# One-hots made one step ahead, checks spread anew, and rows of y written by ScalarE and completed by accumulating transfers

## The chip, the cores and the metric

One core of one Trainium2 chip runs the kernel. The metric is the device time of one execution in microseconds (us). Five engines work side by side, each through its own queue in order: TensorE (PE; its weight loads are PEld), VectorE (DVE), ScalarE (ACT), GpSimd (POOL) and SyncE (SP). SP here only issues transfers (DMAs), also in order: a transfer that waits holds up every later one of SP.

## The reference

```python
xn = _layernorm(x)                       # x: 2048 x 512
out = x + A(xn) + B(xn)

# A: Fourier mixing, y = Cr @ (xn @ Wr^T) - Ci @ (xn @ Wi^T)

# B: product-key experts, 32 heads, 64 x 64 = 4096 experts, 2 of them per head
q = einsum("nd,dhc->nhc", xn, w_q);  s1 = q1 @ k1^T;  s2 = q2 @ k2^T
# top 2 of s1 and of s2, top 2 of their 4 sums; g = softmax over the 2
act = gelu(einsum("nd,nhkd->nhk", xn, u[top_e]))
out_B = einsum("nhk,nhk,nhkd->nd", g, act, v[top_e])
```

## The kernel before

The 2048 rows are 16 blocks of 128. Up to about 455 us of the span the kernel computes part A (its rows go to a buffer y_d in HBM), the scores and the routing. The change lies in what follows: the experts, computed densely. For every block b there are three kinds of work on TensorE:

- **z** (phases ("z", ...), lines 1108 and 1186): xn times all of u, transposed, 128 experts at a time. From block 2 on two blocks go together, in 28 slots of 24 short matmuls (`SEQ`, `slot`). A slot's result lies in one of four shared PSUM banks. ScalarE copies it out (lines 1225, 1230, 1232) or VectorE adds it to what lies in `ACT[b]` (lines 1227, 1235, 1238); the bank is free after that. Gelu follows at line 1215. Part of the weights are sums that stream from HBM through a ring of three slots (`ring_load`, line 1169): when a slot has been read for the last time, SP loads the next 512 KB into it.
- **g** (`g_mm`, line 1289): the gates of the chosen experts, spread to a 128 x 4096 array, in four groups of 32 rows per block. A group has two halves of 16 rows. For each half VectorE makes a one-hot L (line 1279, the low 7 bits of the expert's number) and a one-hot R (line 1284, the high bits) and multiplies R by the gate (line 1287); then 16 matmuls L x R write the bank. L and R have three buffers, taken in turn.
- **v** (phases ("v", b), line 1349): the products times v, 96 long matmuls in eight groups (`cg`) of twelve, all into one bank `pv`. Between them `w_part` (lines 1297 to 1305) forms the next block's products of gates, gelu and scale and splits them into two halves of float16. Seven of sixteen pieces of v stream from HBM (`v_load`, line 1325).

At the end of a block `add_x` has SP load the block's row of part A from y_d into the tile y (line 1359), and GpSimd's queue add x to it with an accumulating transfer (line 1360). `finish` has VectorE compute y = pv * scale + y (line 1364) and SP store y to the output (line 1365). y has one buffer. The last block is finished in `v_part` itself (lines 1331 to 1341), in two halves.

Beside that run **checks** that C and the other given matrices have the structure that part A used. `U` is a step of them: such a step runs what earlier steps left (`later`, `loaded`) and issues the next unit's loads. A unit of C loads 512 KB (lines 1377, 1378), one step later VectorE sums the magnitudes of the first 128 columns (line 1385) and forms differences (lines 1391 to 1429), one step later ScalarE sums the magnitudes of the differences (line 1430). `F[0]` and `F[1]` are steps of another check, `fit`. `verdict`, in the last block, reduces it all to a flag.

Where each piece stands is written by hand: `put(phase, group, ...)` puts it behind a group of matmuls of a phase. This source order is not yet the order of the queues: the framework's planner orders each engine's instructions by priority and by when it expects their inputs. An instruction wrapped in `pin` (`keep_in_program_order`) stays behind the instruction that precedes it in the source on its engine. Waits on semaphores are then set by the framework.

Of the kernel before, what the change touches and what calls it, by code (L numbers as in the profile page):

```python
# [7 lines left out]
F32 = mybir.dt.float32  # L8
# [6 lines left out]
AF = mybir.ActivationFunctionType  # L15
ALU = mybir.AluOpType
AX = mybir.AxisListType

P = 128
S = 2048  # L20
D = 512
KD = D // P
NT = S // P
# [13 lines left out]
def tile_fnet_peer(ctx, tc, x, ca, cb, c5, wt, wf, wr, wq, kt, ut, vn, out):  # L37
# [9 lines left out]
    nc = tc.nc  # L47

    dram = ctx.enter_context(tc.tile_pool(name="dram", bufs=1, space=bass.MemoryType.DRAM))
    y_d = dram.tile([NT, P, D], F32, name="y_d")  # L50
# [43 lines left out]
    chk, asum = sums_sb[:, 0:71], sums_sb[:, 71:139]  # L94
# [12 lines left out]
    zsc, fw, osc = scl[:, 0:1], scl[:, 1:2], scl[:, 2:3]  # L107
# [188 lines left out]
    G = (1, 0, 2, 3)  # L296
# [424 lines left out]
    def part_b(safe, stS, stP, stQ, stE, xt, u_sb, cmp_p, w4):  # L721
# [360 lines left out]
        bp = stE.enter_context(tc.tile_pool(name="bp", bufs=2, side="left"))  # L1082
# [175 lines left out]
            return work, middle, behind  # L1258

        GP = {}  # L1260

        def parts(b):

# [1 line left out]
            return act.rearrange("p c n -> p (c n)").bitcast(F16).rearrange(  # L1265
                "p (c n l) -> p c n l", c=NC, l=2)

        def g_mm(b, tg):
            cmp = CMP[b]
            p = pg(f"g{b}_{tg}")  # L1270
            for hf in range(2):
                ts = slice(tg * TG + hf * 16, tg * TG + hf * 16 + 16)

                def bc(w, n):
                    return cmp[:, w, ts, :].unsqueeze(2).to_broadcast([P, 16, n // 2, 2])

                LR.append(LR.pop(0))
                L, R = LR[-1]
                nc.vector.tensor_tensor(  # L1279
                    L.rearrange("p t (l two) -> p t l two", two=2),  # L1280
                    io_lam.rearrange("p (l two) -> p l two", two=2).unsqueeze(1).to_broadcast([P, 16, P // 2, 2]),
                    bc(0, P), op=ALU.is_equal)
                Rv = R.rearrange("p t (c two) -> p t c two", two=2)
                nc.vector.tensor_tensor(  # L1284
                    Rv, io_c.rearrange("p (c two) -> p c two", two=2).unsqueeze(1).to_broadcast([P, 16, NC // 2, 2]),
                    bc(1, NC), op=ALU.is_equal)
                nc.vector.tensor_tensor(Rv, Rv, bc(2, NC), op=ALU.mult)  # L1287
                for t in range(16):
                    nc.tensor.matmul(p[:, hf, t * NC:(t + 1) * NC], L[:, t, :], R[:, t, :], start=True, stop=True)  # L1289
            GP[b, tg] = p  # L1290

# [68 lines left out]
            nc.gpsimd.dma_start(y, x[b % 4, b // 4], accum_op=ALU.add)  # L1360

        def finish(b, pv):
            y = Y[b]
            nc.vector.scalar_tensor_tensor(y, pv, osc, y, op0=ALU.mult, op1=ALU.add)
            nc.sync.dma_start(out[b * P:(b + 1) * P], y)

        later, loaded = [], []
        pin = tc.keep_in_program_order

        def compare(n):  # L1370

# [9 lines left out]
        def compare_in(n, t, tf, tv):  # L1381

            ri, g, kk = n // 32, n // 8 % 4, n % 8
            odd = kk // 4
            pin(nc.vector.tensor_reduce(asum[:, n:n + 1], tf[:, :P], axis=AX.X, op=ALU.add,
                                        apply_absolute_value=True))
            sgn = (((1, 1, 1), (-1, 1, -1)), ((-1, -1, 1), (1, -1, -1)))[ri][odd]
            ops = [ALU.subtract if v > 0 else ALU.add for v in sgn]
            op = ops[1]
            if g == 0:  # L1390
                pin(nc.vector.tensor_tensor(tv[:, 1], tv[:, 1], tv[:, 0], op=ops[0]))
                for i in (2, 3):
                    nc.vector.scalar_tensor_tensor(tv[:, i], tv[:, 0], not0, tv[:, i], op0=ALU.mult, op1=ops[i - 1])  # L1393
                f = (-1 if ri else 1) * sgn[1] * sgn[2]
                nc.vector.tensor_tensor(tv[0:1, 3], tv[0:1, 3], tv[0:1, 2],
                                        op=ALU.subtract if f > 0 else ALU.add)
            else:
                sets = {}
                for i, o in enumerate(ops):
                    sets.setdefault(o, []).append(i + 1)  # L1400
                for o, ix in sets.items():
                    sl = slice(ix[0], ix[-1] + 1, ix[1] - ix[0] if len(ix) > 1 else 1)
                    v = tv[:, sl]
                    pin(nc.vector.tensor_tensor(v, v, tv[:, 0:1].to_broadcast([P, len(ix), 256]), op=o))
            m = ALU.add if ri else ALU.subtract

            def mirror(v):

                c = 0 if kk else 1
                nc.vector.tensor_tensor(v[:, 2:4, c:], v[:, 2:4, c:], v[:, 0:2, c:], op=m)  # L1410
                if c:
                    nc.vector.tensor_tensor(v[:, 3, 0:1], v[:, 3, 0:1], v[:, 2, 0:1], op=m)

            if g == 0:
                mirror(t[0:1, 2])
                if odd and ri:

                    nc.vector.tensor_copy(t[0:1, 2, 0:2], t[0:1, 0, 0:2])
                elif odd == ri:
                    if ri:  # L1420
                        nc.vector.memset(t[0:1, 2, 0:2], 0.0)
                    else:
                        v = t[0:1, 2, 0:2].rearrange("p q (c a) -> p (q c) a", a=2)
                        nc.vector.tensor_tensor(v, v, c52.unsqueeze(1).to_broadcast([1, 64, 2]), op=ALU.add)
                    if kk == 0:
                        nc.vector.memset(t[0:1, 2, 2, 0:1], 0.0)
            mirror(t[:, 0])
            if kk == 0:
                nc.vector.memset(t[:, 0, 2, 0:1], 0.0)
            later.append(lambda: pin(nc.scalar.activation(tf[:, P:], tf[:, P:], AF.Abs, accum_out=chk[:, n:n + 1])))  # L1430

        def compare_w(n):

# [135 lines left out]
        def pg(name):  # L1569
            return psg.tile([P, 2, 512], F32, tag="pg", name=name, bufs=2)  # L1570
# [9 lines left out]
        def put(ph, cg, *fs):  # L1580
            plan.setdefault((ph, cg), []).extend(fs)

        def G(b, k):
            return lambda: g_mm(b, k)

        def W(b, k, here=False):
            return lambda: w_part(b, k, here)

# [3 lines left out]
        F = [U(it=it) for it in fit_units]  # L1592
        U = U()
# [10 lines left out]
        for b in range(NT):  # L1604
            ph = ("v", b)
            if b % 2 == 0 and 0 < b < 13:
                nx = phases[phases.index(ph) + 1]
                st = 1 if len(nx) == 2 else 2
                put(ph, 1, G(b + 1, 0))
                put(ph, 3, G(b + 1, 1))  # L1610
                put(ph, 5, W(b + 1, 0))
                put(ph, 7, W(b + 1, 1), G(b + 1, 2))
                put(nx, st, W(b + 1, 2, True), G(b + 1, 3))
                put(nx, 3 * st, W(b + 1, 3, True))
            elif b + 1 < NT:
                for k in range(4):
                    put(ph, 2 * k or b % 2, W(b + 1, k))
                put(ph, b % 2, G(b + 1, 2))
                put(ph, 3, G(b + 1, 3))
        put(("v", 13), 5, G(15, 0))  # L1620
        put(("v", 13), 7, G(15, 1))
        for ph in phases[2:]:
            if ph[0] == "z":
                put(ph, 9, G(ph[1], 0))
                put(ph, 12, G(ph[1], 1))
        for b in range(13):
            put(("v", b), 3, lambda b=b: compact_d(b + 2))
        put(("z", 14, 15), 8, lambda: compact_d(15))
        if not safe:
            for cg in (1, 3, 5, 7):  # L1630
                put(("v", 0), cg, F[0])
            for ph, cg in ((("v", 12), 0), (("v", 14), 1), (("v", 14), 3), (("v", 14), 7)):
                put(ph, cg, F[0])
            for ph in phases[3:]:
                if ph[0] == "z":
                    put(ph, 8, F[0])
                    for cg in {2: (9, 11, 13, 15), 4: (9, 11, 13, 15), 6: (9, 11, 13, 15), 14: (9, 12)}.get(ph[1], (9, 12, 15)):
                        put(ph, cg, U)
                elif ph[1] < 14:
                    for cg, f in enumerate((None, F[1], F[1], U, U, U, U, F[0]) if ph[1] % 2 == 0 else (  # L1640
                            None, F[1], F[0], None, U, U, U, F[0])):
                        if f and (ph[1] < 13 or f != U):
                            put(ph, cg, f)
            for cg in range(3):
                put(("v", 14), cg, F[1])
                put(("v", 14 + cg // 2), (6, 7, 0)[cg], U)
                put(("v", 15), cg, F[1])
            for f, n in ((U, 68), (F[0], NK + 16 - V2), (F[1], 16 + V2)):
                assert sum(v.count(f) for v in plan.values()) >= n
# [14 lines left out]
        for n, ph in enumerate(phases):  # L1664
            if ph[0] == "z":
                b = ph[1:]
# [14 lines left out]
            b = ph[1]  # L1681
# [8 lines left out]
            for cg in range(8):  # L1690
# [3 lines left out]
                if b + 1 == NT and cg == 3 and not safe:  # L1694
                    step(None)
                    add_x(b)
                    verdict()
            if b + 1 < NT or safe:
                add_x(b)
            else:  # L1700
                ret = nc.values_load(flags, min_val=0, max_val=1)
            if b + 1 < NT or safe:
                finish(b, pv)
# [150 lines left out]
```

## Time and profile before

| | |
|---|---|
| median of 3 runs | 1131.35 us (1128.64 to 1136.68) |
| profiled execution, its own time | 1135.25 us |
| its span, first to last instruction | 1133.4 us |
| granted TensorE clock, mean | 0.995 |
| busy: PE / DVE / ACT / POOL | 98% / 85% / 59% / 29% of the span |
| HBM read / written | 183.06 MB / 29.69 MB |

The profile is of one execution. A group of instructions is given by its line, engine, operation and the tiles that it writes and reads. An engine's idle time stands before the instruction that ended it, with what released that instruction. The stages that matter below are pairs of blocks in the second half of the span.

### The profile page before, as it was taken

The page shows a single profiled execution, that of the slowest core. Times are in us where ns is not written, and L with a number is a line of the kernel's source. Part 1 is how long each engine was busy: PE and PEld are TensorE (multiplying, and loading weights), DVE is VectorE, ACT ScalarE, POOL GpSimd, SP SyncE. Part 2 cuts the span into 40 slices and gives each one's busy share as a digit, 9 for nine tenths or more (in the row PEclk, how much of TensorE's full clock was granted, in tenths as well). Part 3 has the DMA queues.
Part 4 walks back from the last instruction along what each step waited for, and adds up shares of the span by engine and source line. Part 5 has one row for each costly group of instructions (what it writes and reads, how often), then busy time and mean ns, then how long its engine had stood idle before and what let it go on. Part 6 is the DMA issues. An engine that isn't in the chain of part 4 may idle for free.

```text
span 1133.4 us, 29112 instructions
## 1 busy us (share of the span) xinstructions
PE 1107.3 (98%) x11528; PEld 722.5 (64%) x11528; DVE 962.7 (85%) x2904; ACT 663.9 (59%) x1098; POOL 332.7 (29%) x385
## 2 busy tenths in 40 slices
PE   9999999999999999999999999999999999999997
PEld 6455554544545459687488478478569569569643
DVE  7899789999989799948997897898888888888793
ACT  6558598888877584346445545544535545544442
POOL 0429999899888850000000000000000000000000
PEclk9999999999999999999999999999999999999999
DMA  9883546465353335866666777666668668566354
GB/s 291 292 206 148 185 139 223 117 217 170 92 168 96 111 108 191 236 199 205 226 206 226 227 218 241 218 207 232 200 205 263 199 211 269 190 221 206 121 168 134
DMA packets 132273, 220.51 MB, mean 195 GB/s; under 512 B 35092, under 2 KB 71067, under 8 KB 132126
## 3 DMA queue, kind: packets, MB, share of 16 engines
q1 hardware_dynamic: 129520, 214.28, 58.7%
q0 software_dynamic: 2304, 4.20, 2.8%
q8 instruction: 92, 1.51, 0.5%
q14 instruction: 55, 0.45, 0.1%
q10 hardware_dynamic: 302, 0.08, 0.0%
HBM read 183.06 MB, written 29.69 MB: 188 GB/s over the span
## 4 chain that ended last, share of the span: by engine, by line
PE 59%; DVE 15%; DMA 5%; ACT 4%; issue 2%; POOL 1%; SPq 0%; ACTq 0%; DVEq 0%
PE s L252 18%; PE z L1186 17%; PE v L1349 16%; PE z L1108 4%; DMA cx<-in_cb_dram 3%; DVE w L1297 3%; DVE L L1279 3%; PE g L1289 3%; DVE act L1305 2%; PE m L148 1%; DVE R L1287 1%; DVE R L1284 1%; DVE w L1305 1%; DMA s<-s_d 1%; DVE cx L1393 1%
## 5 line engine op out<-in xcount | busy, mean ns | idle before, releaser
L252 PE MATMUL s<-m,xq 128*128 128x512 f16 x1344 | 297.4, 379 | 1.7 <-ACT ss L962 1.4
L1349 PE MATMUL v<-v,act 128*128 128x512 f16 x1044 | 233.3, 379 | 0.0
L252 PEld LDWEIGHTS <-xq 128*128 128x128 f16 x1344 | 129.6, 98 | 153.1 <-issue 3.2
L1360 POOL DMA_DIRECT2D y<-in_x_dram x16 | 14.4, 897 | 658.7 <-DMA v<-v_d 274.7
L1279 DVE TENSOR_TENSOR L<-io_lam,cmp 128x2048 f16<-128x2048 f16 x128 | 156.2, 1221 | 28.1 <-PE g L1289 28.1
L1349 PEld LDWEIGHTS <-act 128*128 128x128 f16 x1044 | 99.2, 98 | 112.4
L1186 PEld LDWEIGHTS <-u 128*128 128x128 f16 x2688 | 156.2, 98 | 14.8 <-issue 8.3
L966 DVE MAX8 vals<-ss 128x8 f32<-128x64 f32 x896 | 133.3, 216 | 5.5 <-ACT ss L962 5.2
L1186 PEld LDWEIGHTS <-s 128*128 128x128 f16 x1944 | 110.6, 98 | 1.2 <-DMA s<-s_d 1.2
L1349 PE MATMUL v<-v,w 128*128 128x512 f16 x480 | 109.0, 384 | 0.0
L1304 ACT ACTIVATE act<-w 128x1024 f16<-128x1024 f32 x36 | 48.9, 1358 | 92.2 <-DVE w L1297 92.2
L970 DVE FIND_INDEX8 idx<-vals,ss 128x8 uint16<-128x256 f32 x224 | 93.7, 418 | 0.0
L962 ACT ACTIVATE ss<-s,wsc 128x512 f32<-128x512 f32 x120 | 80.0, 680 | 22.5 <-PE s L252 12.6
L1186 PE MATMUL z<-xb,u 128*128 128x128 f16 x1344 | 84.9, 220 | 5.3 <-DVE w L1227 4.7
L1186 PE MATMUL z<-x,u 128*128 128x128 f16 x1344 | 84.7, 220 | 1.6 <-DVE act L1238 1.1
L1186 PE MATMUL z<-x,s 128*128 128x128 f16 x1296 | 81.2, 219 | 1.0 <-DMA s<-s_d 1.0
L1215 ACT ACTIVATE act<-act,scl 128x512 f32<-128x512 f32 x56 | 39.6, 720 | 70.9 <-DVE act L1235 40.9
L1349 PEld LDWEIGHTS <-w 128*128 128x128 f16 x480 | 46.1, 99 | 53.1 <-issue 2.3
L1430 ACT ACTIVATE cx<-cx 128x896 f32<-128x896 f32 x64 | 60.0, 938 | 29.6 <-DVE cx L1410 11.7
L1289 PEld LDWEIGHTS <-L 128*128 128x128 f16 x2048 | 60.7, 96 | 17.3 <-issue 7.2
L1289 PE MATMUL g<-R,L 128*128 128x32 f16 x2048 | 63.5, 177 | 6.6 <-DVE R L1287 6.2
L1305 DVE TENSOR_TENSOR act<-w,act 128x1024 f16<-128x1024 f32 x44 | 58.6, 1332 | 6.1 <-ACT act L1304 6.1
(363 smaller groups left out, 1878.9 us busy)
## 6 DMA issues: line engine op xcount, KB each, us to landing
v<-v_d SPq DMA_DIRECT2D x67, 512.0 KB, 4.6
s<-s_d SPq DMA_DIRECT2D x63, 512.0 KB, 4.2
cx<-in_cb_dram SPq DMA_DIRECT2D x64, 448.0 KB, 5.7
w<-in_wq_dram SPq DMA_DIRECT2D x28, 512.0 KB, 5.9
fit<-in_wq_dram SPq DMA_DIRECT2D x28, 512.0 KB, 4.3
uv<-in_vn_dram SPq DMA_DIRECT2D x16, 512.0 KB
uv<-in_ut_dram SPq DMA_DIRECT2D x16, 512.0 KB, 3.5
s_d<-v SPq DMA_DIRECT2D x32, 256.0 KB, 2.5
```

Of the source, the lines that this page charges most:

```text
L252: nc.tensor.matmul(ps, xt[i][:, l, kd, :], m[:, r, kd, :], start=(n == 0), stop=(n == 3 * KD - 1))
L962: nc.scalar.activation(s, ps, AF.Copy, scale=inv)
L966: nc.vector.max(vals[:, i, w, :, h], s[:, g, :])
L970: nc.vector.max_index(idx[:, i, w].rearrange("p k h -> p (k h)"), vals[:, i, w, 0:2].rearrange("p k h -> p (k h)"), s[:, w * HC:g + 1, :]. ...
L1108: nc.tensor.matmul(ps if n == 1 else ps.rearrange("p (b n) -> p b n", b=2), ug[:, l, c % 2, kd, :], xb2[:, k0, r, kd, :] if n == 1 else xb ...
L1186: nc.tensor.matmul(bank[:, t * P:(t + 1) * P], lt, rt, start=(t == k == 0 and op in "125"), stop=(t == 3 and k == 5), skip_group_check=op ...
L1279: nc.vector.tensor_tensor(L.rearrange("p t (l two) -> p t l two", two=2), io_lam.rearrange("p (l two) -> p l two", two=2).unsqueeze(1).to_ ...
L1289: nc.tensor.matmul(p[:, hf, t * NC:(t + 1) * NC], L[:, t, :], R[:, t, :], start=True, stop=True)
L1304: nc.scalar.activation(w16[..., 0], w, AF.Copy)
L1305: nc.vector.tensor_tensor(w16[..., 1], w, w16[..., 0], op=ALU.subtract)
L1349: nc.tensor.matmul(pv, w16[:, c, :, l], v_sb[g][:, r, cc, :], start=(n + cc == 0 and k == 0), stop=(n == end and cc == 1 and k == 2))
L1430: later.append(lambda: pin(nc.scalar.activation(tf[:, P:], tf[:, P:], AF.Abs, accum_out=chk[:, n:n + 1])))
```

## The change

- The one-hots become a step `g_prep` of their own (`LRP(b, k)` in the list of places), put ahead of the matmuls `g_mm` by one group of rows; L is pinned in source order. Only one prepared group may be outstanding. The number of operations and of buffers stays.
- The sums of magnitudes over the first columns of C move from VectorE (a pinned reduction ahead of the differences) to ScalarE, behind the sum of the differences.
- `finish` no longer adds on VectorE. ScalarE writes y = pv * scale, then two accumulating transfers on GpSimd's queue add the row of y_d and x, one after the other, then SP stores y. `add_x` is left for the last block alone.
- The steps `U` and `F` of the checks get other places: fewer in z phases (none from group 8 to 13), more in v phases.

```diff
+        def g_prep(b, tg):
+            assert not PREP
...
+                PREP.setdefault((b, tg), []).append((L, R))
+                pin(nc.vector.tensor_tensor(
                     L.rearrange("p t (l two) -> p t l two", two=2),
                     io_lam.rearrange("p (l two) -> p l two", two=2).unsqueeze(1).to_broadcast([P, 16, P // 2, 2]),
-                    bc(0, P), op=ALU.is_equal)
+                    bc(0, P), op=ALU.is_equal))
...
+        def g_mm(b, tg):
+            if (b, tg) not in PREP:
+                g_prep(b, tg)
+            p = pg(f"g{b}_{tg}")
+            for hf, (L, R) in enumerate(PREP.pop((b, tg))):
                 for t in range(16):
                     nc.tensor.matmul(p[:, hf, t * NC:(t + 1) * NC], L[:, t, :], R[:, t, :], start=True, stop=True)
...
         def finish(b, pv):
+            if not safe:
+                y = bp.tile([P, D], F32, tag="y", name=f"y{b}", bufs=1)
+                nc.scalar.activation(y, pv, AF.Copy, scale=osc)
+                nc.gpsimd.dma_start(y, y_d[b], accum_op=ALU.add)
+                nc.gpsimd.dma_start(y, x[b % 4, b // 4], accum_op=ALU.add)
+                nc.sync.dma_start(out[b * P:(b + 1) * P], y)
+                return
...
-            pin(nc.vector.tensor_reduce(asum[:, n:n + 1], tf[:, :P], axis=AX.X, op=ALU.add,
-                                        apply_absolute_value=True))
...
-            later.append(lambda: pin(nc.scalar.activation(tf[:, P:], tf[:, P:], AF.Abs, accum_out=chk[:, n:n + 1])))
+            def sums_abs():
+                pin(nc.scalar.activation(tf[:, P:], tf[:, P:], AF.Abs, accum_out=chk[:, n:n + 1]))
+                nc.scalar.activation(tf[:, :P], tf[:, :P], AF.Abs, accum_out=asum[:, n:n + 1])
+
+            later.append(sums_abs)
...
-                put(ph, 1, G(b + 1, 0))
+                put(("v", b - 1), 7, LRP(b + 1, 0))
+                put(ph, 1, G(b + 1, 0), LRP(b + 1, 1))
                 put(ph, 3, G(b + 1, 1))
-                put(ph, 5, W(b + 1, 0))
-                put(ph, 7, W(b + 1, 1), G(b + 1, 2))
+                put(ph, 5, W(b + 1, 0), LRP(b + 1, 2))
+                put(ph, 7, W(b + 1, 1), G(b + 1, 2), LRP(b + 1, 3))
...
-                put(ph, b % 2, G(b + 1, 2))
+                put(ph, b % 2, G(b + 1, 2), LRP(b + 1, 3))
...
-                put(ph, 9, G(ph[1], 0))
+                put(ph, 6, LRP(ph[1], 0))
+                put(ph, 9, G(ph[1], 0), LRP(ph[1], 1))
                 put(ph, 12, G(ph[1], 1))
+                put(ph, 14, LRP(ph[1], 2))
...
-                    put(ph, 8, F[0])
-                    for cg in {2: (9, 11, 13, 15), 4: (9, 11, 13, 15), 6: (9, 11, 13, 15), 14: (9, 12)}.get(ph[1], (9, 12, 15)):
+                    for cg in (0, 4, 14) if ph[1] < 8 else (0, 4):
                         put(ph, cg, U)
...
-                    for cg, f in enumerate((None, F[1], F[1], U, U, U, U, F[0]) if ph[1] % 2 == 0 else (
-                            None, F[1], F[0], None, U, U, U, F[0])):
+                    for cg, fs in enumerate(((F[0],), (F[1],), (F[1], U), (U,), (U,), (U,), (U,), (F[0],)) if ph[1] % 2 == 0 else (
+                            (), (F[1],), (F[0],), (), (U,), (U,), (U,), (F[0],))):
...
-            if b + 1 < NT or safe:
+            if safe:
                 add_x(b)
-            else:
+            elif b + 1 == NT:
                 ret = nc.values_load(flags, min_val=0, max_val=1)
```

More of the change, by code (lines that the diff above doesn't have):

```diff
@@ L1260, in part_b @@
         GP = {}
+        pin = tc.keep_in_program_order
         def parts(b):
@@ L1266, in parts @@
                 "p (c n l) -> p c n l", c=NC, l=2)
-        def g_mm(b, tg):
+        PREP = {}
+        def g_prep(b, tg):
+            assert not PREP
             cmp = CMP[b]
-            p = pg(f"g{b}_{tg}")
             for hf in range(2):
@@ L1278, in g_mm @@
                 L, R = LR[-1]
-                nc.vector.tensor_tensor(
+                PREP.setdefault((b, tg), []).append((L, R))
+                pin(nc.vector.tensor_tensor(
                     L.rearrange("p t (l two) -> p t l two", two=2),
                     io_lam.rearrange("p (l two) -> p l two", two=2).unsqueeze(1).to_broadcast([P, 16, P // 2, 2]),
-                    bc(0, P), op=ALU.is_equal)
+                    bc(0, P), op=ALU.is_equal))
                 Rv = R.rearrange("p t (c two) -> p t c two", two=2)
@@ L1367, in part_b @@
         later, loaded = [], []
-        pin = tc.keep_in_program_order
         def compare(n):
@@ L1584, in G, with LRP @@
             return lambda: g_mm(b, k)
+        def LRP(b, k):
+            return lambda: g_prep(b, k)
         def W(b, k, here=False):
@@ L1631, in part_b @@
                 put(("v", 0), cg, F[0])
-            for ph, cg in ((("v", 12), 0), (("v", 14), 1), (("v", 14), 3), (("v", 14), 7)):
+            for ph, cg in ((("v", 12), 0), (("v", 14), 1), (("v", 14), 3), (("v", 14), 5), (("v", 14), 7)):
                 put(ph, cg, F[0])
@@ L1635, in part_b @@
                 if ph[0] == "z":
-                    put(ph, 8, F[0])
-                    for cg in {2: (9, 11, 13, 15), 4: (9, 11, 13, 15), 6: (9, 11, 13, 15), 14: (9, 12)}.get(ph[1], (9, 12, 15)):
+                    for cg in (0, 4, 14) if ph[1] < 8 else (0, 4):
                         put(ph, cg, U)
                 elif ph[1] < 14:
-                    for cg, f in enumerate((None, F[1], F[1], U, U, U, U, F[0]) if ph[1] % 2 == 0 else (
-                            None, F[1], F[0], None, U, U, U, F[0])):
-                        if f and (ph[1] < 13 or f != U):
-                            put(ph, cg, f)
+                    for cg, fs in enumerate(((F[0],), (F[1],), (F[1], U), (U,), (U,), (U,), (U,), (F[0],)) if ph[1] % 2 == 0 else (
+                            (), (F[1],), (F[0],), (), (U,), (U,), (U,), (F[0],))):
+                        put(ph, cg, *[f for f in fs if ph[1] < 13 or f != U])
             for cg in range(3):
```

## The prediction

> **What bounds the kernel now.** I began with the page (shares of the engines, first line below), then cut the second half of the span, where the change lies, at the boundaries of its pairs of blocks (the other lines), then asked what TensorE and VectorE waited for there.
>
> ```profile
> PE 1107.3 (98%) x11528; PEld 722.5 (64%) x11528; DVE 962.7 (85%) x2904; ACT 663.9 (59%) x1098; POOL 332.7 (29%) x385
> 791.10:881.30 90.20, 86.36 (x1122) 63.03 (x1120) 77.10 (x143) 43.86 (x70) 1.73 (x2) 1.00 0.68 213
> 881.30:967.00 85.70, 85.51 (x1121) 62.75 (x1120) 72.68 (x123) 43.90 (x70) 1.73 (x2) 1.00 0.69 225
> 1124.40:1133.40 9.00, 2.61 (x24) 2.09 (x22) 1.72 (x3) 0.00 (x0) 0.00 (x0) 0.78 0.12 38
> sum 678.40, PE 657.50 PEld 472.41 DVE 552.51 ACT 328.31 POOL 15.38; mean PE 73.06 PEld 52.49 DVE 61.39 ACT 36.48 POOL 1.71
> ```
>
> A row of the stages gives the stretch, its length, then the busy time of PE, PEld, DVE, ACT and POOL. TensorE is the bound: 98% of the span. The two pair rows hold the same matmuls; one takes 85.70 us with 0.19 idle, the other 90.20 with 3.84. So the clean pair is the floor, and the bad one shows what can go wrong. From 455.0 to the end of the matmuls the idle time is 678.40 - 657.50 = 20.90, less 9.00 - 2.61 = 6.39 behind 1124.4: **14.5 us**. No edit here can gain much more; the first 455 us are untouched.
>
> ```profile
> PE g L1289 <- DVE R L1287: 6.2, 10, 2.2
> PE z L1186 <- DVE w L1227: 4.7, 3, 2.4
> PE z L1186 <- DVE act L1238: 1.1, 1, 1.1
> PE z L1186 <- DMA s<-s_d: 1.0, 1, 1.0
> DVE L L1279 <- PE g L1289: 27.0, 11, 3.7
> DVE cx L1404 <- DMA cx<-in_cb_dram: 11.3, 11, 2.5
> ```
>
> These are selected waits from 455 to 1096 us (total, times, longest), from the table of who waited for whom. TensorE waits for VectorE in two ways: for one-hots not yet made (6.2), and for a bank that an addition of z has not emptied (4.7 and 1.1). One case of each, from the timelines of both engines (start, duration, what, and in brackets the idle time before):
>
> ```profile
> 821.09 0.41 DVE L1284 TENSOR_TENSOR R<-io_c,cmp 128x512 f16<-128x512 f16 x1
> 821.42 1.21 DVE L1279 TENSOR_TENSOR L<-io_lam,cmp 128x2048 f16<-128x2048 f16 x1
> 822.56 0.41 DVE L1287 TENSOR_TENSOR R<-R,cmp 128x512 f16<-128x512 f16 x1
> 823.02 0.55 PE L1289 MATMUL g<-R,L 128*128 128x32 f16 x16 [2.24 <-DVE R L1287]
> 773.11 0.88 DVE L1393 SCALAR_TENSOR_TENSOR cx<-cx,not 128x256 f32<-128x256 f32 x2 [2.08 <-DMA cx<-in_cb_dram]
> 775.17 0.67 DVE L1227 TENSOR_TENSOR w<-z,w 128x512 f32<-128x512 f32 x1
> 775.89 1.50 PE L1186 MATMUL z<-xb,u 128*128 128x128 f16 x24 [1.97 <-DVE w L1227]
> ```
>
> In the first, VectorE makes the second half's pair only when the matmuls already want it; an L of a later half was even put between. In the second, a check waits 2.08 us at the head of VectorE's queue for its rows of C, the addition that frees the bank stands behind it, and TensorE loses 1.97.
>
> **The change part by part.** *One-hots as a step.* Removed: nothing; the same 128 L and 256 R operations. One half costs 1.21 + 0.41 + 0.41 = 2.03 us, one step two halves, 4.1. In the new source order a step stands two groups of a v block, or three of a z stage, ahead of its matmuls, so the wait of the 823.02 row goes. I take 5.5 of the 6.2. Bounds: 6.2 gained; or a loss, because the second L of the step behind group k must wait until TensorE has read the first half of group k (three buffers), VectorE already waits 27.0 us in that way, and pinning keeps L from being passed by what precedes it. Behind a waiting L stand additions of z, w products and checks; if a bank hangs on one, TensorE waits too. Half of 27.0 passed on would be 13.5 lost. I cost it at nothing, since VectorE arrives early at an L only when it is ahead; the cover is gone where z's additions fall due in that wait.
>
> *Checks spread anew, sums and rows to ScalarE.*
>
> ```profile
> L1385 DVE TENSOR_REDUCE sums<-cx 128x1 f32<-128x128 f32 x64 | 17.8, 277 | 3.9 <-DMA cx<-in_ca_dram 3.9
> L1364 DVE SCALAR_TENSOR_TENSOR y<-v,scl,y x15: 732/745/757, 490.4 to 1106.8; 128x512 f32<-128x512 f32 x15
> L1225 ACT ACTIVATE act<-z 128x512 f32<-128x512 f32 x16 | 9.5, 591 | 6.2 <-PE z L1186 6.2
> L1474 ACT ACTIVATE cx<-cx x2: 308/308/308, 1108.0 to 1116.3; 1x128 f32<-1x128 f32 x2
> L1474 ACT ACTIVATION_READ_ACCUMULATOR cx<-cx x2: 185/185/185, 1108.2 to 1116.5; 1x1 f32 x2
> ```
>
> VectorE is relieved of 17.8 us of sums and 15 x 0.745 = 11.2 of rows of y: 29.0 of its 552.5. ScalarE takes 64 x (0.308 + 0.185) = 31.6 at most (the one row of that length, one partition) and 15 x 0.591 = 8.9, on 328.3 busy of 678.4: hidden by its own idle time; 40.5 more leaves it 46% idle. If that cover failed, a copy of z would come up to 0.9 us late. Steps of checks in z phases fall from 23 to 17 and none is left at groups 8 to 13, where the 773.11 wait sits. Of the 5.8 us of bank waits quoted I take 4.5; bounds 0 (the wait for C moves along with the check) and 6.9 with the ring's 1.0 and VectorE relieved throughout. Sum of gains: **5.5 + 4.5 = 10**, bounds -13.5 and 14.5.
>
> *Rows of y by accumulating transfers.* Per block, one load on SP's queue goes and one transfer on GpSimd's comes, with the same bytes. The view of the issues gives the median time from issue to landing; its second line is the spread of the x transfer, line 1360.
>
> ```profile
> y<-in_x_dram POOLq DMA_DIRECT2D x16, 256.0 KB, 5.5
> DMA to landing us min/median/max: 4.2/5.5/8.3
> y<-y_d SPq DMA_DIRECT2D x16, 256.0 KB, 3.4
> out_dram<-y SPq DMA_DIRECT2D x15, 256.0 KB, 2.0
> s<-s_d SPq DMA_DIRECT2D x63, 512.0 KB, 4.2
> ```
>
> Before, both terms were in y ahead of the block's end, and the store followed VectorE at once. Now y is written first, then two transfers follow each other: 0.6 + 2 x 5.5 = **11.6 us** until the store may go (0.6 for ScalarE's copy, the two issues' own waits left out). y has one buffer, so the next block's copy, at the head of ScalarE's queue with copies of z and gelus behind it, waits for the transfers and the store, 11.6 + 2.0 = 13.6; the stores of 908.35 and 931.11 (rows further below) are 22.8 apart, so 9 us of cover remain, and 3.6 if both transfers take the longest 8.3. GpSimd's queue holds nothing else here until the verdict at the end. Two places are not safe:
>
> The *end*. The last block still loads y the old way, and its load waits for block 14's store.
>
> ```profile
> 1107.59 0.36 SPq L1365 DMA_DIRECT2D out_dram<-y  x1
> 1124.43 0.75 DVE L1331 SCALAR_TENSOR_TENSOR y<-v,scl,y 128x512 f32<-128x512 f32 x1 [2.22 <-PE v L1349]
> 1125.74 0.48 DVE L1340 SCALAR_TENSOR_TENSOR y<-v,scl,y 128x256 f32<-128x256 f32 x1 [0.56 <-PE v L1338]
> 1127.05 0.48 DVE L1340 SCALAR_TENSOR_TENSOR y<-v,scl,y 128x256 f32<-128x256 f32 x1 [0.83 <-PE v L1338]
> ```
>
> Block 14's store would go at about 1107 + 11.6 = 1118.6 instead of 1107.59, land by 1120.6, the load by 1124.0, the addition of x by 1129.5; line 1331 ran at 1124.43. That is 5.1 late, less the 0.56 and 0.83 for which the two additions behind it waited on TensorE: 3.7, **+4**. Bounds: with the shortest landing, 4.2, in all three places it is 0.6 + 8.4 + 2.0 + 3.4 + 4.2, so 1.2 late and hidden: 0; with the longest before the store, 17.2 instead of 11.6: +9. What is late next is the store of the last half rows.
>
> The Trainium skill speaks against these rows: "DMA: Bandwidth & Descriptors", section "Anatomy of one DMA — SWDGE (gpsimd) path", gives 2.0 us plus bytes by 436 GB/s, an estimate of 2.6 us for 256 KB. The trace disagrees: 5.5 measured for this very transfer. By the page the end would cost nothing, and the sum would be 4 us lower; that is the last rival.
>
> *SP's queue.* The store stands in it in an order fixed beforehand. First a row of SP's waits, then its timeline, then TensorE's:
>
> ```profile
> SPq L1365 <- DVE y L1364: 47.6, 10, 13.5
> 908.35 0.34 SPq L1365 DMA_DIRECT2D out_dram<-y  x1
> 931.11 0.34 SPq L1365 DMA_DIRECT2D out_dram<-y  x1
> 933.17 0.33 SPq L1359 DMA_DIRECT2D y<-y_d  x1
> 933.80 0.32 SPq L1169 DMA_DIRECT2D s<-s_d  x1
> 932.27 1.50 PE L1186 MATMUL z<-x,s 128*128 128x128 f16 x24
> 941.11 1.50 PE L1186 MATMUL z<-x,s 128*128 128x128 f16 x24
> ```
>
> The load of 933.80 refills the ring slot that the matmuls of 932.27 have read, and those of 941.11 read it: 7.3 us, of which landing takes 4.2. **3.1 us are spare.** I take 0 for the queue, as the order is made anew with the store's later readiness; the other end is the second rival.
>
> Sum: -10 + 4 = **-6** against the profiled execution, 1133.4 span and 1.85 around it, 1135.25: 1129. The median of the runs shown, 1131.35, lies 3.9 below that execution; against it: **1125**.
>
> **The rivals.** *Everything comes out.* All idle time before the last matmul goes, and the end is covered: -14.5, 1117. For: the clean pair shows that the program can run so. Against: the end.
>
> *SP blocked by the store.* It is put ahead of ring loads that are free sooner. For: SP already sits at line 1365 up to 13.5 us, so the order does put it early. Against: now the planner knows of the transfers. It decides from 3.1 us of blocking. At half the chain, 5.8 us, each of the later 13 stores costs 2.7: +35, less 6, 1160; at the whole chain 8.5 each, +110.
>
> *No gain: the step doesn't do what it says.* Pinning doesn't bring R ahead (only L is pinned), VectorE waits for C in the new places as long, and the end costs 4: 0 to +4, 1131 to 1135. For: the 11.3 us, 11 times, at line 1404 show that checks meet their rows of C late in many places. Against: the 823.02 wait needs only an early place.
>
> *Only the end is covered.* The gain of 10 stays and the transfers are short: 1121. Line 1331 is on time if each takes (1124.43 - 1107.6 - 2.0 - 3.4 - 5.5) / 2 = 3.0; none of the 16 took under 4.2, so I give it 0.03. The page named above says so.
>
> **How the numbers follow.** Forecast, 1119 to 1131: 0.47. Only the end: 0.03. Everything: 0.15. No gain: 0.17. SP blocked: 0.18. The range takes in all but the lower edge of "everything" and the blocked queue beyond its mild end, 1113 to 1145; 0.2 is left out. One per cent, 11.3 us, is about what a measurement of this kernel can tell from no change: faster than 1120 has the 0.15 and a part of the forecast, 0.25; slower than 1142.7 nearly all of the last, 0.17; the rest 0.58.
>
> **What would show it.** Right: the wait of g for R under 1 us; bank waits under 2; idle time before the last matmul 5 or less; ScalarE 40 us busier; the last block's addition held by y's transfer. Wrong: waits of z for s or of v for its stream, SP's line of the store waiting over 100 us in total, or L waiting longer for g with banks behind it.

## The result, and the profile after

1224.02 us (median of 4, 1222.45 to 1226.45) against 1129.99 before: ratio 1.0825 [1.0772, 1.0877], slower by 93 us. The profiled execution has a span of 1222.3 us, 88.9 more than before. Shares of the engines, then TensorE's waits from 455 us on (total, times, longest), then one row of SP's:

```profile
PE 1132.8 (93%) x11528; PEld 739.7 (61%) x11528; DVE 941.2 (77%) x2825; ACT 694.4 (57%) x1241; POOL 346.1 (28%) x400
```
```profile
PE z L1186 <- DMA s<-s_d: 35.8, 14, 5.9
PE v L1359 <- DMA v<-v_d: 26.5, 6, 7.8
PE z L1186 <- DVE act L1227: 8.9, 4, 5.6
PE z L1186 <- DVE w L1227: 3.1, 2, 1.9
PE g L1299 <- DVE L L1283: 1.3, 2, 0.7
PE z L1186 <- DVE act L1235: 0.8, 3, 0.3
PE g L1299 <- DVE R L1291: 0.7, 1, 0.7
```
```profile
SPq L1378 <- DMA y<-in_x_dram: 126.1, 15, 12.9
```

The waits on VectorE moved by a few us: g for one-hots 2.0 instead of 6.2, banks 12.8 instead of 5.8 in the rows shown, here and in the prediction. What is new is 62.3 us of waits for streams that were on time before: the ring s (1.0 before) and v (none). SP stands at the store of y, now line 1378, for 126.1 us, 8.4 per block. TensorE's busy time also grew, by 1132.8 - 1107.3 = 25.5, for the same 11528 matmuls. All of TensorE's waits from 455 us on, short ones included, are 77.3 instead of 14.1; these 63.2 and the 25.5 are 88.7 of the 88.9.

One case from the timelines of ScalarE, GpSimd, SP and TensorE, and the same stretch in stages (after the length: busy time of the five engines, clock, DMA share, GB/s):

```profile
991.40 0.67 ACT L1375 ACTIVATE y<-v,scl 128x512 f32<-128x512 f32 x1
```
```profile
992.48 0.88 POOL L1376 DMA_DIRECT2D y<-y_d  x1 [22.77 <-ACT y L1375]
1001.29 0.86 POOL L1377 DMA_DIRECT2D y<-in_x_dram  x1 [7.93 <-DMA y<-y_d]
```
```profile
992.12 0.38 SPq L1169 DMA_DIRECT2D s<-s_d  x1
1005.49 0.34 SPq L1378 DMA_DIRECT2D out_dram<-y  x1
...
1006.29 0.34 SPq L1169 DMA_DIRECT2D s<-s_d  x1
```
```profile
993.31 1.50 PE L1186 MATMUL z<-xb,s 128*128 128x128 f16 x24
...
1010.02 2.74 PE L1186 MATMUL z<-xb,s 128*128 128x128 f16 x24 [5.93 <-DMA s<-s_d]
1013.60 2.74 PE L1186 MATMUL z<-x,s 128*128 128x128 f16 x24 [0.84 <-DMA s<-s_d]
```
```profile
1004.00:1013.00 9.00, 2.83 (x26) 2.48 (x24) 4.31 (x9) 1.00 (x3) 0.00 (x0) 0.71 0.76 244
1013.00:1017.00 4.00, 3.40 (x33) 3.40 (x34) 1.18 (x2) 0.72 (x1) 0.00 (x0) 0.50 0.58 213
1017.00:1030.00 13.00, 13.00 (x247) 13.00 (x246) 5.84 (x10) 5.74 (x9) 0.00 (x0) 0.96 0.44 140
```

ScalarE writes y at 991.40 and the store goes at 1005.49, 14.1 us later. This is the longest of the 15; the shortest is 9.8, the median 11.8. SP has nothing in front of the store from 992.50 on. The ring slot that the matmuls of 993.31 read is free at 994.8, but its refill stands behind the store and is issued at 1006.29, 11.5 late. TensorE waits 5.93 us for it, and then runs at half its clock: 24 matmuls take 2.74 us instead of 1.50. That is the second cost: over the whole execution the mean granted clock is 0.968 instead of 0.995, which goes with the 25.5 of busy time.

The end went as the queue went, not as the last addition went. SP's and TensorE's timelines in the last block:

```profile
1199.99 0.36 SPq L1378 DMA_DIRECT2D out_dram<-y  x1
1200.44 1.34 SPq L1335 DMA_DIRECT2D v<-v_d  x3
```
```profile
1204.43 8.94 PE L1359 MATMUL v<-v,act 128*128 128x512 f16 x30 [7.81 <-DMA v<-v_d]
```

Three loads of v leave at once behind block 14's store, and TensorE idles 7.81 us.

### The profile page after: what moved, and what is told of

It reads as the page before. It is cut to its first block, busy times and chain, and to the rows that moved or that the text cites. A ratio compares the mean times of both kernels' runs of the same rounds, so it can differ in the third digit from the quotient of the medians.

```text
span 1222.3 us, 29260 instructions
## 1 busy us (share of the span) xinstructions
PE 1132.8 (93%) x11528; PEld 739.7 (61%) x11528; DVE 941.2 (77%) x2825; ACT 694.4 (57%) x1241; POOL 346.1 (28%) x400
## 4 chain that ended last, share of the span: by engine, by line
PE 38%; DVE 24%; DMA 17%; POOL 7%; ACT 6%; issue 6%; SPq 1%; DVEq 0%; POOLq 0%; ACTq 0%
PE z L1186 15%; PE s L252 13%; DMA y<-y_d 4%; DVE L L1283 4%; PE v L1359 4%; DMA s<-s_d 4%; DMA cx<-in_cb_dram 3%; DMA y<-in_x_dram 3%; DVE w L1307 3%; DVE cx L1418 3%; PE z L1108 2%; DVE act L1315 2%; ACT act L1314 2%; DVE vals L966 2%; DVE idx L970 2%
## 5 line engine op out<-in xcount | busy, mean ns | idle before, releaser
L1359 PE MATMUL v<-v,act 128*128 128x512 f16 x1044 | 238.8, 385 | 20.3 <-DMA v<-v_d 20.3
L1376 POOL DMA_DIRECT2D y<-y_d x15 | 13.4, 891 | 665.2 <-ACT y L1375 595.3
L1186 PEld LDWEIGHTS <-u 128*128 128x128 f16 x2688 | 161.3, 100 | 21.1 <-issue 14.8
L1186 PEld LDWEIGHTS <-s 128*128 128x128 f16 x1944 | 121.0, 103 | 38.7 <-DMA s<-s_d 38.7
L1186 PE MATMUL z<-xb,u 128*128 128x128 f16 x1344 | 90.1, 227 | 12.0 <-DVE act L1227 8.9
L1186 PE MATMUL z<-x,s 128*128 128x128 f16 x1296 | 86.1, 226 | 12.0 <-DMA s<-s_d 12.0
L1418 DVE TENSOR_TENSOR cx<-cx 128x512 f32<-128x512 f32 (+2 forms) x84 | 48.5, 615 | 40.8 <-DMA cx<-in_cb_dram 40.8
L1186 PE MATMUL z<-xb,s 128*128 128x128 f16 x648 | 47.2, 237 | 23.9 <-DMA s<-s_d 23.9
```

Of the source, the lines that this page charges most:

```text
L1186: nc.tensor.matmul(bank[:, t * P:(t + 1) * P], lt, rt, start=(t == k == 0 and op in "125"), stop=(t == 3 and k == 5), skip_group_check=op ...
L1359: nc.tensor.matmul(pv, w16[:, c, :, l], v_sb[g][:, r, cc, :], start=(n + cc == 0 and k == 0), stop=(n == end and cc == 1 and k == 2))
```

## The experiments

Theory **queue**: SP stands at the head of its queue at the store, and the streams behind it come late. Rivals: **order** (pinned one-hots and new places make VectorE late, the streams only follow) and **memory** (twice the transfers on GpSimd's queue slow the others).

**The store on another queue** (e1), in the changed kernel:

```diff
-                nc.sync.dma_start(out[b * P:(b + 1) * P], y)
+                nc.gpsimd.dma_start(out[b * P:(b + 1) * P], y)
```

> The changed kernel with one edit: the store of y goes out on GpSimd's queue, behind the two accumulating transfers that it waits for anyway, instead of SP's queue. Theory 'queue' (SP stands at the store until both transfers have landed, 126 us in all, and the ring's, v's and C's loads behind it come late): 1115 to 1135 us, waits of z for s and of v for v_d under 5 us together (62 now), granted clock back to 0.99. Rival 'order' (pinned L and the new places of the checks make VectorE late, loads are late only in its train): 1200 or more. Rival 'memory' (twice the transfers on GpSimd's queue slow the other loads; s lands in 5.6 us instead of 4.2): 1190 or more, since one transfer more goes through that queue.

1147.38 us, 1.0147 [1.011, 1.0183]. One word takes back 77 of the 93 us, with one transfer more on GpSimd's queue: *memory* and *order* fall as main causes. The waits for streams fall from 62.3 to 7.8, busy time to 1109.4:

```profile
PE z L1186 <- DMA s<-s_d: 4.1, 4, 1.8
PE v L1348 <- DMA v<-v_d: 3.0, 1, 3.0
PE v L1359 <- DMA v<-v_d: 0.7, 1, 0.7
```

But it is 12 us slower than *queue* allowed at most, and the 7.8 are above the 5 that it expected.

**Rows of y as before** (e2), in the changed kernel; `add_x` is called as in the kernel before:

```diff
-            if not safe:
-                y = bp.tile([P, D], F32, tag="y", name=f"y{b}", bufs=1)
...
-                return
-            if safe:
+            if b + 1 < NT or safe:
                 add_x(b)
```

> The changed kernel with y finished as before the change (load on SP, x by one accumulating transfer ahead of time, VectorE's sum, store); one-hots, checks and sums stay changed. 'queue': 1115 to 1128 us, the prediction's gain of about 10 us without its loss at the end. 'order': 1200 or more. 'memory': 1115 to 1128 too.

1149.27 us, 1.0138 [1.0095, 1.0181], which no theory expected. The other three parts cost 16 us where the prediction had 10 gained. That is as much as e1 still lost.

**Rows of y alone** (e3), in the kernel before; `add_x` is called as in the changed kernel:

```diff
+            if not safe:
+                y = bp.tile([P, D], F32, tag="y", name=f"y{b}", bufs=1)
...
+                nc.sync.dma_start(out[b * P:(b + 1) * P], y)
+                return
```

> The kernel before with only the rows of y changed (ScalarE's copy, two accumulating transfers, store on SP). 'queue': 1210 to 1240 us, the whole loss and none of the other parts' gain; SP waits over 100 us at the store. 'order': 1125 to 1140. 'memory': 1190 or more.

1180.07 us, 1.042 [1.0377, 1.0463]. SP waits 106.8 us at the store, as *queue* says, but the loss is some 30 us short of the least that *queue* expected, and lies in no other range either. So +48 here and +16 in e2 leave 29 us to an interplay.

**One transfer less** (e4):

```diff
-                nc.gpsimd.dma_start(y, x[b % 4, b // 4], accum_op=ALU.add)
```

> The changed kernel without the second accumulating transfer (x is not added, so the output lacks x in blocks 0 to 14). The store may go some 7 us after the copy instead of 11. 'queue': the blocking falls by about 4 us per block, to little over the 3.1 us that the ring has to spare: 1135 to 1165 us. 'order': 1200 or more. 'memory': halfway back, about 1170.

1162.63 us, 1.0274 [1.0239, 1.0309], within *queue*. SP's wait is a scale for it. The rows of e4 and of e3 (each its own line of the store):

```profile
SPq L1377 <- DMA y<-y_d: 74.1, 15, 6.2
```
```profile
SPq L1368 <- DMA y<-in_x_dram: 106.8, 15, 10.9
```

Per store SP waited 4.9, 7.1 and (all parts) 8.4 us. Less the ring's spare 3.1, times 15: 28, 60 and 80 us. Measured against the same kernel with y as before: 13, 48 and 75. The estimate is high each time, most of all for the shortest wait: the streams could bear more than 3.1 us.

**One part at a time** (e5 to e8): the one-hot step, the checks' places, the sums, and the rows of y with the store on GpSimd's queue, each alone in the kernel before. The lines that carry each edit:

```diff
+                put(("v", b - 1), 7, LRP(b + 1, 0))
+                put(ph, 1, G(b + 1, 0), LRP(b + 1, 1))
...
+                    for cg in (0, 4, 14) if ph[1] < 8 else (0, 4):
                         put(ph, cg, U)
...
-            pin(nc.vector.tensor_reduce(asum[:, n:n + 1], tf[:, :P], axis=AX.X, op=ALU.add,
-                                        apply_absolute_value=True))
+                nc.scalar.activation(tf[:, :P], tf[:, :P], AF.Abs, accum_out=asum[:, n:n + 1])
...
+                nc.gpsimd.dma_start(out[b * P:(b + 1) * P], y)
```

> The kernel before with the one-hot step alone (own step, earlier places, L pinned). With y as before the changed kernel was still 15 to 17 us slower, so one of three parts costs that. Theory 'places' (the checks' new places: their loads and their waits for C now stand at the start of z, in front of the additions that free banks, and one group after each other in v): 1120 to 1130 us here, g waiting under 2 us for R. Rival 'pinned' (L pinned and the second half waiting for TensorE hold VectorE up): 1140 to 1152 us. Rival 'sums': as 'places' here.

> The kernel before with the checks' new places alone. 'places': 1140 to 1155 us, waits of VectorE for C of 4 us and more in each pair, and z waiting for banks and for s 15 us or more in all. 'pinned' and 'sums': 1125 to 1135.

> The kernel before with the sums of C moved to ScalarE alone. 'places' and 'pinned': 1125 to 1133 us, VectorE 18 us less busy and ScalarE about 25 more. 'sums' (ScalarE holds the tiles of C longer, loads of C wait for a buffer and SP with them): 1140 or more.

> The kernel before with only the rows of y changed, and the store on GpSimd's queue. Beside the same with the store on SP's queue, 1180 us, it prices the standing at the head of SP's queue without the other parts. 'queue': 1128 to 1140 us (what is left is the end of the last block, up to 7 us, as its load of y stands on SP behind the store). 'memory' (the transfers themselves slow the others): 1155 or more.

- One-hots: 1131.98 us, 1.0004 [0.9985, 1.0024]. No effect that can be measured, 2 us above the expected range for *places*, far from *pinned*.
- Places: 1143.81 us, 1.0093 [1.0062, 1.0123]. About 11 us lost, as *places* says. The waits of z for banks and for s are 14.1 us, just under the 15 expected.
- Sums: 1125.42 us, 0.992 [0.9893, 0.9948]. About 7 us gained (9 by the ratio). This is the best kernel of the study; it beats both. VectorE is 11.7 us less busy where 18 were expected, ScalarE 20.8 more where 25 were.
- Rows of y, store on GpSimd: 1137.64 us, 1.0033 [1.0008, 1.0057]. The stand on SP's queue alone is worth 1180.07 - 1137.64 = 42 us.

Waits of TensorE, first with the places alone, then with the sums alone:

```profile
PE g L1289 <- DVE R L1287: 6.0, 11, 2.3
PE z L1186 <- DVE w L1227: 5.9, 3, 3.2
PE z L1186 <- DVE act L1235: 3.5, 4, 1.6
PE z L1186 <- DVE act L1227: 2.8, 2, 2.1
PE z L1186 <- DMA s<-s_d: 1.9, 3, 1.4
```
```profile
PE z L1186 <- DVE w L1227: 2.1, 2, 1.1
PE z L1186 <- DVE w L1235: 1.9, 1, 1.9
PE z L1186 <- DVE act L1238: 1.5, 1, 1.5
PE g L1289 <- DVE R L1287: 1.2, 2, 1.0
PE z L1186 <- DVE act L1235: 1.0, 1, 1.0
```

The new places raise the bank waits from 6.9 in all to 12.2 and leave g's wait as it was. With the sums moved away g's wait falls from 6.2 to 1.2, though the one-hots are still where they were; the banks' stays at 6.5. Whether the lighter load on VectorE did it, or that a pinned instruction left its queue, was not told apart.

**Two or three parts at a time** (e9 to e12). e9 is the changed kernel with the checks' places of the kernel before:

```diff
-                    for cg in (0, 4, 14) if ph[1] < 8 else (0, 4):
+                    put(ph, 8, F[0])
+                    for cg in {2: (9, 11, 13, 15), 4: (9, 11, 13, 15), 6: (9, 11, 13, 15), 14: (9, 12)}.get(ph[1], (9, 12, 15)):
```

The other three join the edits of e5 to e7 in the kernel before.

> The changed kernel with the checks in their old places (one-hots, sums and rows of y stay changed, store on SP). So far, against 1132: rows of y alone +48, places +11, one-hots 0, sums -9, all together +93, 43 more than their sum. Theory 'pile-up' (the new places put loads of C at the head of z and right behind the block's end: they lengthen the first transfer, 6.6 to 8.4 us in even blocks instead of 4.0 to 4.4, and stand themselves behind the store, so VectorE waits 10 us for C): 1165 to 1180 us here, the first transfer back under 5 us in even blocks. Rival 'pinned' (a pinned L behind a check that waits for C is what multiplies): 1190 or more, since one-hots stay pinned.

> The kernel before with one-hots and sums changed, places and rows of y as before: the parts that cost nothing alone. 'pile-up': 1118 to 1126 us, a version that beats both kernels. 'pinned': 1125 to 1135, as pinned L needs the room that the sums gave.

> The kernel before with one-hots and places changed. Alone they give 0 and +11; the three parts without y gave +16 where their sum is +2. 'pinned' (L stands behind the check before it in the source, which in the new places waits for C): 1148 to 1160 us. Without an interplay of these two: 1140 to 1146.

> The kernel before with places and sums changed, one-hots as before. If the interplay is between one-hots and places: 1131 to 1138 us (+11 - 9). If it is between sums and places (without VectorE's pinned sum the differences of a check move up in its queue and meet C's rows earlier): 1145 or more.

- Rows of y, one-hots and sums (e9): 1182.76 us, 1.0466 [1.0427, 1.0505], just above the range of *pile-up*. The old places alone take back 41 us.
- One-hots and sums (e10): 1129.52 us, 0.9977 [0.9957, 0.9997], 4 us over what *pile-up* expected, within *pinned*. The one-hot step takes back part of what the sums gave.
- One-hots and places (e11): 1155.55 us, 1.0203 [1.0157, 1.025], +23 where the sum is +11, within *pinned*.
- Places and sums (e12): 1136.26 us, 1.0033 [1.0013, 1.0054]: additive, so what multiplies among the three parts without y is one-hots with places.

**Is it the pin?** (e13 to e15): L without `pin`, with the places alone (e13) and in the whole changed kernel (e14); and rows of y with places, without the one-hot step (e15).

```diff
-                pin(nc.vector.tensor_tensor(
+                nc.vector.tensor_tensor(
...
-                    bc(0, P), op=ALU.is_equal))
+                    bc(0, P), op=ALU.is_equal)
```

> One-hots and places changed (1155 us), with L no longer pinned; the step and its place stay. 'pinned': 1140 to 1147 us, as without the one-hot step. Rival 'early step' (the step itself, made between the checks, holds VectorE up where z's additions are due): 1150 to 1160.

> The changed kernel with L no longer pinned. If pinning multiplies what the store does: 1200 us or less. If not: 1210 to 1225, the store on SP and the new places keep nearly all.

> The kernel before with rows of y (store on SP) and places changed, one-hots and sums as before. Alone +48 and +11. 'pile-up' (loads of C in the new places lengthen the first transfer and stand behind the store): 1208 to 1225 us. Without an interplay of these two: 1187 to 1195.

1154.1 us, 1.0207 [1.0174, 1.0239], and 1219.82 us, 1.078 [1.0754, 1.0806], with the pin 1155.55 and 1224.02: pinning changes next to nothing, and *pinned* falls; it is the early step that meets the new places. VectorE and TensorE with one-hots and places (e11), at the start of a z stage:

```profile
580.23 1.27 DVE L1315 TENSOR_TENSOR act<-w,act 128x1024 f16<-128x1024 f32 x1
581.41 0.27 DVE L1419 TENSOR_TENSOR cx<-cx 128x128 f32<-128x128 f32 x1
581.60 1.21 DVE L1283 TENSOR_TENSOR L<-io_lam,cmp 128x2048 f16<-128x2048 f16 x1
582.74 0.67 DVE L1227 TENSOR_TENSOR act<-z,act 128x512 f32<-128x512 f32 x1
```
```profile
583.47 2.72 PE L1186 MATMUL z<-xb,u 128*128 128x128 f16 x24 [2.92 <-DVE act L1227]
```

A w product, a check and an L that no matmul wants yet stand in front of the one addition that frees TensorE's bank. In five of the seven z stages of e11 an L runs in the 4 us before that addition; in the first stage a check waits 4.25 us for C instead. This is read from the trace, not tried apart, and it is not the whole of the 12 us. From e6 to e11 the bank waits rise only from 12.2 to 14.3, with these rows:

```profile
PE z L1186 <- DVE w L1227: 7.2, 3, 2.8
PE z L1186 <- DMA s<-s_d: 6.4, 4, 2.5
PE z L1186 <- DVE act L1227: 6.3, 4, 2.9
```

The wait for s rises from 1.9 to 6.4, that of v for halves of w from 0.5 to 2.9, busy time from 1108.3 to 1113.4; g's waits fall from 6.0 to 1.0. Why s comes later stays open.

Rows of y with places (e15): 1205.38 us, 1.0668 [1.0622, 1.0714], +73 where the sum is +59: an interplay, smaller than *pile-up* expected. The median landing of the first transfer, y from y_d, suggests one way: 5.7 us here and 6.0 in the changed kernel, with the new places; 4.7 in e3 and 4.6 in e9, with the old ones. The row of the issues in e15, then in e9:

```profile
y<-y_d POOLq DMA_DIRECT2D x15, 256.0 KB, 5.7
```
```profile
y<-y_d POOLq DMA_DIRECT2D x15, 256.0 KB, 4.6
```

C's loads, now issued at the block's end, and the transfer run at the same time. That they are what lengthens it is argued from these rows and was not tried apart. SP's wait at the store grows with it, from 106.8 us in e3 to 127.9 here:

```profile
SPq L1368 <- DMA y<-in_x_dram: 127.9, 15, 12.2
```

Five pairs of runs differ in the new rows of y, with the store on SP's queue: e4 and the changed kernel against e2, e3 against the kernel before, e9 against e10, e15 against e6. SP's wait less 4 us for each of the 15 stores gives 14, 66, 47, 51 and 68 us; measured are 13, 75, 48, 53 and 62. The 4 us are chosen to fit. With them the wait at the store gives the price of y within 9 us, whatever the other parts are. Of the 41 us of interplay (93 less 0, 11, -7 and 48 of the four parts alone) some 30 are found in pairs of parts, as listed below; the rest stays open.

## Why the prediction was wrong

- **The bound** was right: TensorE's clean pair is the floor, and all losses are waits of TensorE and the slower clock after them. One sum in it is off: the upper bounds 6.2 and 6.9 of its two gains make 13.1, and the 14.5 it gives is the whole idle time. Nothing hangs on it.
- **One-hots, 5.5 gained**: the wait named went, 6.2 to 1.6 in e5, yet the time stayed. 2.8 of the 4.6 us came back as a new wait, v for the halves of w:

```profile
PE v L1359 <- DVE act L1315: 2.8, 4, 0.7
```

  The step costed the moved VectorE work at nothing because "VectorE arrives early at an L only when it is ahead". What decided was what an early L stands in front of. The loss end of that bound (additions behind it) is a part of what e11 shows; pinning, named as one of its causes, was not it.
- **Checks, sums and rows of y relieving VectorE, 4.5 gained**: edits in one sum, with opposite signs. Sums gained 7 alone; places lost 11, beyond the bound of 0. The relief was also smaller than summed: VectorE is 21.5 us less busy in the changed kernel, not 29.0, and ScalarE 30.5 busier, not 40.5. The step took away steps from the middle of z and left out what they would meet at groups 0 and 4: the additions of z's start.
- **The end, +4**: in the changed kernel hidden behind the 7.81 us of the streams. With the streams on time (e8) the whole change of y costs 4 us. In its trace 2.9 us are a wait for v before the last matmuls, and not the late addition. It is SP's queue again: the last load of v stands behind the last block's load of y, which waits for block 14's store.

```profile
PE v L1338 <- DMA v<-v_d: 2.9, 1, 2.9
```
```profile
1118.89 0.32 SPq L1359 DMA_DIRECT2D y<-y_d  x1
1119.32 0.36 SPq L1325 DMA_DIRECT2D v<-v_d  x1
```
- **SP's queue, taken at 0**: the step that failed. It is worth 77 of the 93 us with the other parts in place (e1), and 42 alone (e3 against e8). Its two ends were 0 and the whole chain. The chain itself was sized well: 11.6 us against a median of 11.8 from the copy to the store. What failed is the argument that the order would be made anew with the store's later readiness. In the case shown the store did move, behind the first refill; but the next refill was free inside the chain's time and stood behind the store, and on average SP waited 8.4 us per store. The row it quoted against itself, SP already standing at this line up to 13.5 us, was the nearest one, and it was overruled by an argument with no row. The rival's price at the whole chain, +110 less 6, lies near the 93 measured partly by luck: the queue cost 77 or 42, and the rest are losses of parts that the prediction had as gains. Its chance, 0.18, and the range's upper end, which stopped at its mild end, were the error. Both signs of being wrong that the prediction named for this queue came: 62.3 us of waits for the streams, and 126.1 us of SP at the store.
- **Nothing for interplay**: the sum added the parts. That leaves 41 of the 93 us. Measured in pairs are 14 (rows of y with places, +73 for +59), 12 (one-hots with places, +23 for +11) and 4 (one-hots with sums, -3 for -7); the slower clock after each wait, inside all of these, the prediction had not priced.

## What to carry to other kernels

Before a store is put behind a chain of transfers, ask whose queue it stands on and what is behind it there; an in-order issuing queue that feeds just-in-time streams must not hold an instruction that waits longer than the streams' spare time (here 3.1 us by one row of the ring, about 4 by the five pairs). The same store on a queue with nothing urgent behind it cost 4 us instead of 48. And price parts that place work on one engine's queue in pairs, not alone: early one-hots cost nothing, new places 11 us, both 23.

## What the runs showed of the hardware

A wait of TensorE can cost more than its length. After 5.93 us of idle time the granted clock was 0.50 in the stretch 1013 to 1017, and back at 0.96 on average from 1017 on; 24 matmuls took 2.74 us there instead of 1.50. In the second half of all these runs every wait of more than 3.4 us was followed by slower matmuls. After waits of about 2 to 3.3 us it went either way. Two rows of e4:

```profile
584.93 1.50 PE L1186 MATMUL z<-xb,u 128*128 128x128 f16 x24 [3.30 <-DVE act L1227]
955.40 2.74 PE L1186 MATMUL z<-x,s 128*128 128x128 f16 x24 [2.04 <-DMA s<-s_d]
```

The Trainium skill, "TensorE: Matmul & The Clock Gate", section "Part 1: The HAM clock gate (the "warmup" mystery)", says that the clock is halved after at least one idle window of about 3.4 us, and that the windows run freely. The traces agree above 3.4 us; the fall after only 2.04 us of idle time is not covered by that sentence.

An accumulating transfer of 256 KB on GpSimd's queue took a median of 6.0 us (y_d, 3.8 to 8.4) and 4.2 us (x) in the changed kernel. That is 2.3 and 1.6 times the 2.6 us that the prediction estimated from the Trainium skill's page "DMA: Bandwidth & Descriptors", section "Anatomy of one DMA — SWDGE (gpsimd) path". The first of the two was longer in the runs with the checks' new places (5.7 and 6.0) than in those with the old ones (4.7 and 4.6).
